# Diagonal matrices from GpSimd to VectorE, weight remainders to GpSimd, a third place for scores, contiguous q, k, v, and another order, in a fused attention and gated feed-forward kernel

## The chip, the core and the metric

The kernel runs on one core of a Trainium2 chip. A core has TensorE (PE: matmuls; PEld is its weight load), VectorE (DVE), ScalarE (ACT), GpSimd (POOL) and SyncE (SP, which here issues nearly all DMAs). The metric is the device time of one execution in microseconds. Three runs of the kernel before gave 413.46, 413.92 and 414.34 us.

## The reference

Three layers follow each other: windowed attention (4 batches, 8 heads, 576 positions, 64 wide; each query sees itself and the 63 keys before it), a token-shift feed-forward layer with a gate, and a convolution-gated layer.

```python
scores = scale * np.matmul(q, k.transpose(0, 1, 3, 2))
mask = (rel >= 0) & (rel < window)                 # window = 64
scores = np.where(mask, scores, -1000000000.0)
scores = scores - np.max(scores, axis=-1, keepdims=True)
attn = np.exp(scores)
attn = attn / (np.sum(attn, axis=-1, keepdims=True) + 1e-09)
x = np.matmul(attn, v)                             # then heads side by side: (4, 576, 512)

xk = mu_k * x + (1.0 - mu_k) * x_prev              # x_prev: x one position earlier
xr = mu_r * x + (1.0 - mu_r) * x_prev
k = np.maximum(xk @ w_k, 0.0)                      # 512 -> 1024
x = 1.0 / (1.0 + np.exp(-(xr @ w_r))) * (k * k @ w_v)

gate_pre += conv_w[k] * xp[:, k:k + S, :]          # 5 taps
x = (sigmoid(gate_pre) * (x @ w_val)) @ w_out
```

## The kernel before

The 2304 positions are cut into five blocks: block 0 of 256 and blocks 1 to 4 of 512. Attention runs in units: one block and one pair of heads, so four units a block, 0 to 3 for block 0, 4 to 7 for block 1, and so on. x lies with its features across partitions (tile xT).

A unit of block 0 takes these steps. The scores (qk, PE) come with the mask added by small matmuls of the tile low. DVE takes each row's maximum (top), ACT the exponentials and their sums (exp), POOL or DVE adds 1e-9 (eps), DVE takes the reciprocal (rec). A diagonal matrix of the reciprocals is made from the identity (diag, L446 to L455): as one DVE instruction over 4x128 columns (L453) or as four POOL instructions of 128x128 (L451). A matmul with it transposes and scales the weights (tp, L499), a copy brings them to SBUF (pt, L505, L506), a matmul with v gives the output (pv, L513), and a copy puts it into xT (x, L462, L463). Later units mask with DVE and a small memset on POOL (edge, L571), scale with norm (L442, L439) and transpose on DVE (tr).

The mixed inputs of block 0 are made by ACT (a) and DVE (xm, L643), for r and for k, in two groups of two head pairs. The products r, h (its relu squared) and v follow on PE: for block 0 in plain f32 from the weights' own words (L706), for blocks 1 to 4 as three products of halves: a weight is rounded (hi, L372, L373), and the remainder (lo, L375) is the difference of the weight and its rounded half. Weights come as 64-bit words in ten pieces (w_r two, w_k four, w_v four) that each need g (ACT, L351), t and s (DVE, L354, L356), hi and lo, all on 128x1024 elements. Block 0 needs a piece's s; blocks 1 to 4 need hi and lo. The last layer follows, by Strassen's scheme for three of four batches.

The table SLOT gives each operation its place in one order for the whole kernel, and a letter (v, a, p) the engine where there is a choice (v is DVE, a ACT, p POOL). Each engine's instructions, and SP's DMAs, stand in that order, so an engine that waits holds up all that it has later in the order. Plan.run goes through the order with a model of times, which decides one thing only: where it thinks that PE would idle before the first product it puts in filler matmuls (fill; the L1272 instructions).

In PSUM, the scores of units 0 to 4 take turns in two places (p0), and unit 5 has a third (s4). Products of later stages take over p0's banks at pg, when the exponentials of units 0 to 4 are done.

Of the kernel before, what the change touches and what calls it, by code (L numbers as in the profile page):

```python
# [20 lines left out]
P = 128  # L21
# [22 lines left out]
    'first': '0',  # L44
    'warm': '1',
    'cap': '3',
    'ident': '2',
    'band': '13',
    'low': '4',
    'table': '12',  # L50
    'ldmu': '7',
    'ldc': '92',
    'mu': '51',
    'omu': '52',
    'pg': '79',
    'wc0': '323 250 326',
    'wc': '327',
    'first_x': '6',
    'ldqk': '8 9 10 14 16 49 101 127 161 150 195 256 328 338 367 414 406 433 461 528',
    'ldv': '15 30 60 68 87 110 139 181 289 235 305 322 386 390 432 453 507 505 550 607',  # L60
    'qk': '18 21 22 36 45 69 103 148 187 241 257 337 350 373 389 431 452 508 520 540',
    'top': '19 23 29 53 62 77 140 178 262 267 283 347 366 404 422 443 460 524 541 554',
    'exp': '20 25 33 55 71 78 147 191 269 281 297 355 375 408 428 454 468 531 552 557',
    'eps': 'v24 p26 v41 p59 p88 p112 p175 p192 v270 v282 v311 p365 v380 v410 p439 v464 p488 p543 p558 p565',
    'rec': '27 35 50 64 91 138 176 198 271 285 312 368 381 411 447 466 516 544 568 583',
    'diag': 'v28 p40 p57 p67',
    'tp': '34 44 61 73',
    'pt': 'v37 a46 v66 v82',
    'pv': '38 48 70 83 128 166 200 223 294 313 356 378 412 436 481 499 535 563 573 614',
    'x': 'v47 a56 v81 a84 a136 a182 a216 a238 v298 a317 a357 v384 v415 v444 a486 a502 a536 a567 a578 a643',  # L70
    'norm': 'v95 v154 v179 v215 v272 v306 a340 a371 a382 a426 v448 v495 v517 v545 v569 v595',
    'tr': '96 158 184 219 273 308 348 372 399 427 449 496 533 551 572 604',
    'mask': '107 160 194 246 274 344 354 374 405 434 459 513 534 553',
    'edge': '126 171 218 264 280 345 360 376 413 437',
    'a': 'a65 a85 a89 a113 a225 a228 a244 a248 a333 v334 a392 v393 a465 v471 a521 v523 a605 a610 a686 v711',
    'xm': '75 98 108 114 236 237 277 251 349 346 403 395 478 476 547 538 622 663 690 738',
    'xlo': '76 100 137 120 240 243 321 255 364 391 441 397 512 518 587 577 677 708 724 783',
    'carry': '118 123 278 295 363 420 522 570',
    'r': '80 105 86 121 93 119 102 116 336 339 342 352 462 483 501 494 655 695 681 692 801 824 826 827',
    'sig': '115 124 129 135 341 358 370 388 477 487 515 519 676 696 697 698 816 825 837 838',  # L80
    'h': '149 153 146 159 143 151 145 152 169 177 174 189 185 196 183 197 290 287 268 279 296 307 314 302 '
        '416 435 407 421 450 467 463 479 599 594 600 611 618 613 667 653 749 748 778 766 780 784 804 818',
    'relu': 'a155 a163 a157 a162 a204 a205 a206 a210 a291 a292 a286 a293 v318 v320 a331 a332 a442 a451 a429 '
        'v430 a474 a485 v484 a497 a602 v603 v617 a624 a649 v657 a668 v669 a756 v758 a779 a791 a793 v796 '
        'a817 a821',
    'sbuf': '164 165 208 211',
    'slo': 'a202 a203 a209 a212 310 325 330 353 472 480 503 510 629 642 684 679 792 808 829 828',
    'v': '220 230 213 233 226 253 254 259 359 383 361 377 401 417 400 402 525 555 537 561 566 580 514 532 '
        '712 735 699 710 706 720 747 752 866 884 831 851 843 853 860 882',
    'x2': '263 247 258 260 387 379 425 409 559 571 588 564 742 723 733 763 892 888 887 889',  # L90
    'st': '276 284 369 303 418 398 445 473 575 584 630 582 769 743 772 774 950 959 1000 987',
    'xhi': 'a239 a242 v319 v252 v362 v385 v440 a396 a511 a500 a576 a546 a672 v700 a716 v757',
    'cut': '232 249 343 394 475 530',
    'shi': '300 315 324 335 456 457 491 498 621 625 660 670 762 795 797 822',
    'sq': 'a301 a316 v329 a351 v469 a470 a492 v506 v628 a627 a683 a678 a777 v805 a819 v823',
    'staging': '5',
    'w_r ld': '11 42',
    'w_r g': '32 58',
    'w_r t': '31 63',
    'w_r s': '39 72',  # L100
    'w_r hi': 'a43 v90',
    'w_r lo': '54 94',
    'w_k ld': '104 74 125 131',
# [12 lines left out]
    'turn': '836',
    'turn_s': '895',
    'turn_w': '865 845',
    'w_val ld': '542 562 597 647',
    'w_val room': '585 631 615 646',  # L120
    'w_val g': '586 633 619 654',
    'w_val t': '590 593 601 596 606 581 635 637 636 638 612 644 651 626 652 659 665 673 682 680',
    'w_val s': '592 634 620 661',
    'w_val hi': 'v608 a639 v662 a688',
    'w_val lo': '609 645 671 691',
    'w_val st': '616 632 648 658 666 675 717 705',
    'w_out ld': '640 694 740 746',
    'w_out room': '674 703 744 786',
    'w_out g': '687 704 745 787',
    'w_out t': '713 715 718 722 719 702 729 730 732 750 770 775 785 781 788 755 800 806 807 810',  # L130
    'w_out s': '714 721 771 798',
    'w_out hi': 'a726 v760 v789 a813',
    'w_out lo': '736 761 790 815',
    'w_out st': '759 751 767 773 809 802 814 835',
    'wv2': '867 839',
    'wo2': '902 880 881 848',
    'ldx': '841 904 926 1001',
    'gbuf': '871 922 1040 1034',
    'ldg': '873 949 1043',
    'xhi_': 'a846 v883 v855 a852 a879 a877 a910 a925 a909 a923 a948 a940 a972 a1056 a966 a982 a1002 a1009 a1075 '  # L140
        'a1106 a1077 a1090 v1124 v1105',
    'xlo_': '847 899 856 858 900 878 916 962 915 928 953 946 981 1061 991 983 1035 1021 1080 1118 1096 1102 '
        '1138 1110',
    'xsum': '842 849 859 876 906 911 924 934 958 964 994 1007 1070 1088 1103 1104',
    'val': '885 886 898 901 905 912 914 919 927 935 944 954 974 980 989 1066 999 1008 1028 1073 1044 1086 1098 '
        '1109 1114 1120 1135 1146',
    'valu': 'a891 a903 a907 a929 a945 a960 a996 a1016 a1031 a1100 a1112 a1127',
    'valc': '893 913 917 921 933 965 975 993 1068 1039 1082 1054 1108 1130 1140 1165',
    'gv': '894 920 918 932 973 978 986 1011 1069 1067 1089 1055 1164 1157 1142 1170',
    'ghi_': 'v896 a936 a930 a939 a943 a956 a967 a995 a1012 a1004 a992 a1006 a1022 a1025 a1093 a1062 a1101 v1113 '  # L150
        'a1116 v1144 a1132',
# [1179 lines left out]
```

## Time and profile before

| | |
|---|---|
| median of three runs | 413.92 us |
| the profiled execution: time, span | 413.41 us, 411.5 us |
| PE busy, share of the span | 402.6 us, 98% |
| DVE | 340.5 us, 83% |
| ACT | 261.5 us, 64% |
| POOL | 38.3 us, 9% |
| chain that ended last, by engine | PE 95%, POOL 3%, DVE 1% |
| moved by DMA | 78.37 MB |

The time of an execution is longer than its span, which runs from the first instruction on an engine to the last. A matmul's end is modelled, so that a busy PE is not a PE at its peak. Granted clock is the share of TensorE's full 2.4 GHz that the throttle allows. Idle time of an engine costs something only where another engine waits for it.

### The profile page before, as it was taken

Reading aid. Unit: us, or ns where it says so; the run is one execution under the profiler, and the core shown is the slowest. Engines: PE = TensorE matmul, PEld = TensorE weight load, DVE = VectorE, ACT = ScalarE, POOL = GpSimd, SP = SyncE. Lnnn points to the kernel's source line nnn. Section 1 sums busy time; section 2 is a strip of 40 time slices with the busy share of each in tenths; the row PEclk is TensorE's granted clock in tenths of the full one; section 3 lists DMA queues with packets and bytes.
Section 4 is the critical chain, followed back from the end, with each engine's and each line's share of the span. In section 5 each row is a group of like instructions: output and inputs, shape, how many; then the busy total and the mean of one; then the engine's idle time right before and its main releaser. Section 6 shows DMA issues by size and latency. Waiting matters only on the chain.

```text
span 411.5 us, 10921 instructions
## 1 busy us (share of the span) xinstructions
PE 402.6 (98%) x4587; PEld 342.1 (83%) x4587; DVE 340.5 (83%) x503; ACT 261.5 (64%) x607; POOL 38.3 (9%) x87
## 2 busy tenths in 40 slices
PE   8899999999999999999999999999999999999995
PEld 4678888887778778877888888888888999999995
DVE  4899999798548489789898899788885999999960
ACT  4889995778884767686556653156322476977531
POOL 3920101000100011000000000000000001123110
PEclk9999999999999999999999999999999999999999
DMA  7998911214323342262266428564999727869664
GB/s 284 411 414 339 328 46 57 78 44 145 107 74 129 98 125 77 78 223 92 80 242 263 149 89 291 208 235 156 405 395 382 261 86 245 228 142 198 137 149 128
DMA packets 24674, 78.37 MB, mean 190 GB/s; under 512 B 3376, under 2 KB 6704, under 8 KB 21808
## 3 DMA queue, kind: packets, MB, share of 16 engines
q1 hardware_dynamic: 22608, 72.64, 48.8%
q0 software_dynamic: 1872, 5.01, 7.3%
q8 instruction: 36, 0.59, 0.6%
q14 instruction: 14, 0.11, 0.1%
q10 hardware_dynamic: 144, 0.00, 0.0%
HBM read 51.80 MB, written 23.49 MB: 183 GB/s over the span
## 4 chain that ended last, share of the span: by engine, by line
PE 95%; POOL 3%; DVE 1%; ACT 0%; issue 0%; ACTq 0%; POOLq 0%
PE v L683 22%; PE h L683 21%; PE r L683 11%; PE sv L596 5%; PE h L706 4%; PE v L706 4%; PE sv L551 3%; PE val1m L961 3%; PE val3m L961 3%; PE out L1073 3%; PE out2m L961 3%; PE out1m L961 3%; PE val2m L961 3%; PE out0m L961 3%; PE val0m L961 3%; POOL rk L451 2%
## 5 line engine op out<-in xcount | busy, mean ns | idle before, releaser
L683 PE MATMUL h<-x,wk 128*128 128x512 f32 x384 | 90.5, 392 | 0.0
L683 PEld LDWEIGHTS h<-x,wk 128*128 128x128 f32 x384 | 71.6, 188 | 15.0
L683 PE MATMUL v<-sh,wv 128*128 128x512 f32 x256 | 82.4, 394 | 0.0
L683 PEld LDWEIGHTS v<-sh,wv 128*128 128x128 f32 x256 | 48.0, 188 | 10.8
L427 ACT ACTIVATE s<-s,m 128x96 f32<-128x96 f32 x120 | 43.0, 362 | 12.6 <-DVE m L416 11.5
L683 PE MATMUL v<-sl,wv 128*128 128x512 f32 x128 | 49.9, 390 | 0.0
L683 PE MATMUL r<-x,wr 128*128 128x512 f32 x192 | 45.8, 393 | 0.0
L683 PEld LDWEIGHTS r<-x,wr 128*128 128x128 f32 x192 | 35.7, 188 | 7.8
L892 DVE SCALAR_TENSOR_TENSOR early<-early,wc 128x576 f32<-128x576 f32 x48 | 38.5, 813 | 3.2 <-ACT early L890 2.7
L733 ACT ACTIVATE rk<-h 128x512 f32<-128x512 f32 (+1 forms) x30 | 15.4, 534 | 25.4 <-PE h L683 21.9
L683 PEld LDWEIGHTS v<-sl,wv 128*128 128x128 f32 x128 | 24.0, 188 | 4.7
L596 PEld LDWEIGHTS sv<-pt,vt 32*64 32x64 f32 x1536 | 18.9, 130 | 6.0 <-issue 3.9
L427 ACT ACTIVATION_READ_ACCUMULATOR s<-s,m 128x1 f32 x120 | 22.8, 190 | 0.0
L643 DVE SCALAR_TENSOR_TENSOR xm<-xT,omu,xm 128x512 f32<-128x512 f32 x32 | 22.3, 745 | 0.4 <-POOL xT L649 0.3
L666 DVE TENSOR_TENSOR x<-xm,x 128x1024 fp32r<-128x1024 f32 x16 | 19.5, 1219 | 3.6 <-ACT x L663 3.5
L785 DVE TENSOR_TENSOR sgs<-v,sgs 128x512 f32<-128x512 f32 (+1 forms) x20 | 12.5, 633 | 11.5 <-PE v L683 10.9
L763 DVE TENSOR_TENSOR sl<-rk,sh 128x1024 fp32r<-128x1024 f32 x16 | 19.5, 1221 | 2.4 <-ACT rk L761 2.2
L596 PE MATMUL sv<-pt,vt 32*64 32x32 f32 (+2 forms) x1536 | 20.8, 238 | 0.3 <-issue 0.3
L584 DVE STREAM_TRANSPOSE pt<-s 128x768 f32<-128x768 f32 x16 | 15.6, 973 | 5.1 <-ACT s L439 4.8
L757 ACT ACTIVATE sh<-rk 128x1024 fp32r<-128x1024 f32 x16 | 16.8, 1055 | 1.0 <-DVE rk L735 0.9
L896 ACT ACTIVATE early<-early 128x1152 f32<-128x1152 f32 x6 | 7.0, 1169 | 15.8 <-DVE early L892 15.8
L773 ACT ACTIVATE sgs<-r 128x512 f32<-128x512 f32 (+1 forms) x20 | 10.5, 552 | 8.2 <-PE r L683 8.1
(212 smaller groups left out, 828.0 us busy)
## 6 DMA issues: line engine op xcount, KB each, us to landing
qk<-qk SPq DMA_DIRECT2D x16, 544.0 KB, 5.1
vt<-vh SPq DMA_DIRECT2D x16, 384.0 KB, 3.9
xb<-x2d SPq DMA_DIRECT2D x4, 1152.0 KB, 6.7
out_t<-st SPq DMA_DIRECT2D x15, 288.0 KB, 2.9
w_out<-w SPq DMA_DIRECT2D x8, 512.0 KB, 3.4
w_val<-w SPq DMA_DIRECT2D x8, 448.0 KB, 3.1
wk<-w_val SPq DMA_DIRECT2D x2, 1792.0 KB, 8.8
early<-x2d SPq DMA_DIRECT2D x6, 576.0 KB, 4.4
```

The costliest lines, as they stand in the source:

```text
L427: ACT.activation(out=s, in_=scores()[:, 2 * c // n_s, c % (n_s // 2), :] if scores else s, func=AF.Exp, scale=D ** -0.5 if scores else 1.0 ...
L584: V.transpose(out=a["pt"][:, :m2 * KW], in_=a["s"].rearrange("p c j -> p (c j)"))
L596: PE.matmul(a["o"][heads[h], i, j0 * HW:j1 * HW], lhsT=a["v"][r, k, heads[h]], rhs=p, start=k == 0, stop=k == m + 1, skip_group_check=True)
L643: V.scalar_tensor_tensor(out=m, in0=xT[:, f, :n], scalar=omu[:, c:c + 1], in1=m, op0=ALU.mult, op1=ALU.add)
L666: lambda E: E.tensor_tensor(out=dst(1), in0=src(), in1=f32(dst(0)), op=ALU.subtract))
L683: PE.matmul(ps, lhsT=a, rhs=b[:, kt, :], start=(kt == 0 and i == 0), stop=(kt == nk - 1 and i == 2))
L706: PE.matmul(Ps[key][:, :n], lhsT=ws(kt), rhs=x()[:, kt, :], start=kt == 0, stop=kt == nk - 1)
L733: ACT.activation(out=o, in_=ps, func=AF.Relu)
L757: ACT.activation(out=Ss[t][0][:, f, :n], in_=rk(), func=AF.Square)
L763: lambda E: E.tensor_tensor(out=Ss[t][1][:, f, :n], in0=rk(), in1=f32(Ss[t][0][:, f, :n]), op=ALU.subtract))
L892: V.scalar_tensor_tensor(out=o, in0=x, scalar=c, in1=o, op0=ALU.mult, op1=ALU.add)
L961: PE.matmul(z[bank][:, j, :HS], lhsT=lhs, rhs=rhs, start=new and kt == 0 and e == 0, stop=kt == 1 and e == 2, skip_group_check=not new)
```

## The change

All four diagonals are made on DVE (the code offers ACT instead; the order takes DVE). lo may stand on POOL, and does for six of the ten pieces. The scores of the six early units go through three places in turn, p0, p0 and s4, by the unit's number; so unit 2 goes to s4, and unit 5 follows it there. pg then waits for the exponentials of units 0 and 3 alone, and the third and fourth r tile for those of 1 and 4. tp no longer waits for pv of the unit before; the copy pt does. Fillers write to the tp or pv places. The host lays out q with k, and v, so that what a unit loads is one contiguous stretch of memory; each DMA moves the same bytes to the same partitions. And nearly every place in SLOT is new. Of the table four entries are shown.

```diff
-    'ldqk': '8 9 10 14 16 49 101 127 161 150 195 256 328 338 367 414 406 433 461 528',
+    'ldqk': '9 11 12 15 16 64 82 102 146 170 252 260 306 362 353 374 382 440 477 509',
-    'diag': 'v28 p40 p57 p67',
+    'diag': 'v27 v42 v49 v62',
-    'w_r lo': '54 94',
+    'w_r lo': 'p69 p116',
-    'w_k lo': '180 144 227 229',
+    'w_k lo': 'v224 p203 p232 v226',
...
-    RAMP, STALL = 3500, 1300
+    STALLS = ((3500, 2000), (17500, 1100))
...
-        vg((key, "lo"), n, [(key, "hi")],
-           lambda E: E.tensor_tensor(out=dst[1], in0=s(), in1=f32(dst[0]), op=ALU.subtract))
+        rest = lambda E: E.tensor_tensor(out=dst[1], in0=s(), in1=f32(dst[0]), op=ALU.subtract)
+        plan.any((key, "lo"), [(key, "hi")], ("dve", v_ns(n), lambda: rest(V)), ("pool", 8000, lambda: rest(G)))
...
+    def unit_rows(a, o, hp, n):
+        return a[o + hp * P * n:][:P * n].rearrange("(p n) -> p n", p=P)
...
-            o = 2 * t0 + W * t
-            DMA.dma_start(out=both[:, :2 * n + W], in_=qkh[hp, :, o:o + 2 * n + W])
+            DMA.dma_start(out=both[:, :2 * n + W], in_=unit_rows(qkh, HP * P * (2 * t0 + W * t), hp, 2 * n + W))
...
+        def by_act():
+            d = diag()
+            for c in range(n_s):
+                ACT.activation(out=d[:, c], in_=ident, func=AF.Copy, scale=l(1)[:, c:c + 1])
         plan.any(("diag", u), [("rec", u), "ident", *free],
-                 ("pool", 1300, lambda: [G.tensor_scalar(out=o, in0=ident, scalar1=l(1)[:, c:c + 1], scalar2=None, op0=ALU.mult)
-                                         for o in [diag()] for c, o in enumerate([o[:, c] for c in range(n_s)])]),
+                 ("act", 290 * n_s, by_act),
...
+    def space(u):
+        return Q["s4"] if u % 3 == 2 else p0.tile([P, 2, TB], F32, tag="p0", name=f"qk{u}")
...
-            a["ps"] = p0.tile([P, 2, TB], F32, tag="p0", name=f"qk{u}")
+            a["ps"] = space(u)
...
-        op(("tp", u), "pe", 870, [("diag", u), *([("pv", u - 1)] if u else [])], tp, ring=("pa", ("pt", u)))
+        op(("tp", u), "pe", 870, [("diag", u)], tp, ring=("pa", ("pt", u)))
...
-        plan.any(("pt", u), [("tp", u)],
+        plan.any(("pt", u), [("tp", u), *([("pv", u - 1)] if u else [])],
...
-    op("pg", "none", 0, [("exp", u) for u in range(HP + 1)], products)
+    op("pg", "none", 0, [("exp", 0), ("exp", 3), After(("exp", 1)), After(("exp", 4))], products)
...
-        if "pg" in Q:
-            if "spare" not in Q:
-                Q["spare"] = Q["pg"].tile([P, TB], F32, tag="g", name="spare")
-            ps = Q["spare"]
-        elif "ps" not in A[HP + 1]:
-            ps = Q["s4"][:, 0]
-        elif len(held) < 2:
-            ps = Q["pv" if "tp" in held else "tp"]
-        else:
+        if "sv" in Q or len(held) > 1:
             return
+        ps = Q["pv" if "tp" in held else "tp"]
```

On POOL, from the masks of the start on, the order before is this (first_m and m4, m5 are the sums to which eps adds, rk the diagonals, s6 and s7 the scores whose mask is finished by memsets):

```order
L324 COPY band_96<-cap_95 32x96 x4
L432 TENSOR_SCALAR first_m_99<-first_m_99 128x4
L451 TENSOR_SCALAR rk_71<-ident_58,first_m_99 128x128 x8
L432 TENSOR_SCALAR first_m_99<-first_m_99 128x4
L451 TENSOR_SCALAR rk_71<-ident_58,first_m_99 128x128 x4
L432 TENSOR_SCALAR m4_364<-m4_364 128x8
L432 TENSOR_SCALAR m5_449<-m5_449 128x8
L571 MEMSET s6_549 32x2x64
L571 MEMSET s6_549 32x2x32
L571 MEMSET s7_711 32x2x64
L571 MEMSET s7_711 32x2x32
```

At the same place on POOL the new order has (wr1 and wk1 are the remainders of w_r and w_k; s8 is the next unit's mask):

```order
L442 TENSOR_SCALAR first_m_99<-first_m_99 128x4 x3
L331 COPY band_96<-cap_95 32x96 x4
L442 TENSOR_SCALAR m4_323<-m4_323 128x8
L381 TENSOR_TENSOR wr1_66<-words_119,wr0_65 128x4x256
L587 MEMSET s6_539 32x2x64
L587 MEMSET s6_539 32x2x32
L381 TENSOR_TENSOR wr1_66<-words_119,wr0_65 128x4x256
L587 MEMSET s7_667 32x2x64
L587 MEMSET s7_667 32x2x32
L381 TENSOR_TENSOR wk1_64<-words_119,wk0_63 128x4x256
L665 MEMSET xT_100 128x2
L587 MEMSET s8_832 32x2x64
```

The twelve diagonal instructions are gone from POOL, and remainders stand between the memsets of successive units.

On DVE, the last instructions ahead of the first mixing pair (the one that the first r product needs; rk is a diagonal, tp the transposed weights, words and x, s here the weight pieces, m the maxima of a later unit) are before:

```order
L375 TENSOR_TENSOR wr_66<-words,wr_65 128x4x256
L418 TENSOR_REDUCE m_364<-qk_285 128x8
L419 TENSOR_SCALAR m_364<-m_364 128x8
L354 TENSOR_SCALAR s_140<-s_140 128x1024
L435 RECIPROCAL first_m<-first_m 128x4
L506 COPY pt_359<-tp 128x512
L356 SCALAR_TENSOR_TENSOR words<-words,s_140 128x1024
L643 SCALAR_TENSOR_TENSOR x_139<-xT,omu,x_139 128x256 x2
```

The new order of DVE ends there with these:

```order
L466 TENSOR_TENSOR rk<-ident,first_m 128x512
L522 COPY pt_331<-tp 128x512
L361 TENSOR_SCALAR x_117<-x_117 128x1024
L445 RECIPROCAL first_m<-first_m 128x4
L363 SCALAR_TENSOR_TENSOR words<-words,x_117 128x1024
L478 COPY xT<-pv 128x256
L380 CAST wr_65<-words 128x4x256
L466 TENSOR_TENSOR rk<-ident,first_m 128x512
L428 TENSOR_REDUCE m_440<-s_143 128x8
L429 TENSOR_SCALAR m_440<-m_440 128x8
L659 SCALAR_TENSOR_TENSOR x_117<-xT,omu,x_117 128x256 x2
```

The diagonals (L466) are on DVE ahead of the pair, the remainder of the first w_r piece and the words of the second are no longer there, and the maxima of unit 5 (m_440) are.

On SP, which issues the loads, the first DMAs are before (x_139 and s_140 are the places of the two w_r pieces, early and qk units' q and k, sgs and rk their v):

```order
L400 DMA early<-qk 128x576 x3
L369 DMA x_139<-w_r 128x2048
L400 DMA early<-qk 128x576
L406 DMA sgs<-vh 128x512
L400 DMA qk_154<-qk 128x1088
L406 DMA sgs<-vh 128x512
L369 DMA s_140<-w_r 128x2048
```

And in the new order:

```order
L410 DMA early<-qk 128x576 x4
L410 DMA qk_173<-qk 128x1088
L415 DMA sgs<-vh 128x512
L376 DMA x_117<-w_r 128x2048
L415 DMA rk<-vh 128x512
L415 DMA sgs<-vh 128x512
L410 DMA qk_375<-qk 128x1088
L376 DMA s_118<-w_r 128x2048
```

The first w_r piece has moved behind the loads of units 3 and 4 and the first v.

## Rows read from the trace of the kernel before

**Rows 1.** Stages: PE, PEld, DVE, ACT, POOL busy us (x), PEclk, DMA, GB/s.
```profile
10.00:15.00 5.00, 4.24 (x105) 3.00 (x108) 4.82 (x11) 3.89 (x12) 4.39 (x5) 1.00 1.02 414
15.00:20.00 5.00, 4.35 (x149) 3.24 (x136) 3.58 (x6) 5.00 (x24) 4.54 (x7) 1.00 1.03 408
20.00:25.00 5.00, 4.57 (x49) 3.55 (x44) 4.82 (x10) 3.91 (x25) 2.23 (x4) 1.00 1.03 420
...
50.00:60.00 10.00, 10.00 (x227) 8.48 (x227) 9.84 (x11) 9.72 (x15) 0.12 (x2) 1.00 0.27 89
```

**Rows 2.** The chain that ended last, in order of time: start us, us, what.
```profile
10.61 2.67 POOL rk L451 x3
...
13.82 3.93 POOL rk L451 x4
...
18.41 3.63 POOL rk L451 x4
...
22.08 0.49 PE tp L499 x2
22.57 0.86 PE r L706 x4
23.43 0.62 PE pv L513 x16
...
26.84 0.93 PE sv L551 x56
...
42.01 0.30 issue
...
69.72 10.92 PE h L683 x48
```

**Rows 3.** Timeline of PE, first product: start, us, engine, line, op, tiles, count.
```profile
22.40 0.38 PE L706 MATMUL r<-x,words 128*128 128x256 f32 x1
```

**Rows 4.** Groups by line and form, POOL, 0 to 70 us: busy us, mean ns.
```profile
L451 POOL TENSOR_SCALAR rk<-ident,first_m 128x128 f32<-128x128 f32 x12 | 10.8, 911 | 1.4 <-DVE first_m L435 1.1 <-PE tp L499 0.4
...
L432 POOL TENSOR_SCALAR first_m<-first_m 128x4 f32<-128x4 f32 x2 | 0.4, 196 | 5.3 <-ACT xm L427 5.2
```

**Rows 5.** The same groups of DVE, 0 to 70 us.
```profile
L375 DVE TENSOR_TENSOR wk<-words,wk 128x1024 fp32r<-128x1024 f32 x4 | 4.8, 1211 | 0.0
...
L354 DVE TENSOR_SCALAR words<-words 128x1024 int32<-128x1024 int32 x4 | 2.7, 690 | 0.0
...
L356 DVE SCALAR_TENSOR_TENSOR words<-words,x 128x1024 int32<-128x1024 int32 x2 | 2.4, 1217 | 0.0
...
L506 DVE COPY pt<-tp 128x512 f32<-128x512 f32 x3 | 2.0, 682 | 0.2
...
L418 DVE TENSOR_REDUCE m<-qk 128x8 f32<-128x768 f32 x1 | 1.0, 959 | 0.5 <-PE qk L551 0.5
...
L453 DVE TENSOR_TENSOR rk<-ident,first_m 128x512 f32<-128x512 f32 x1 | 0.7, 691 | 0.0
```

**Rows 6.** Timeline of POOL, two of the twelve diagonal instructions.
```profile
12.67 0.60 POOL L451 TENSOR_SCALAR rk<-ident,first_m 128x128 f32<-128x128 f32 x1
...
18.98 1.64 POOL L451 TENSOR_SCALAR rk<-ident,first_m 128x128 f32<-128x128 f32 x1
```

**Rows 7.** Timeline of DVE, beside the second of those.
```profile
18.93 1.22 DVE L356 SCALAR_TENSOR_TENSOR words<-words,s 128x1024 int32<-128x1024 int32 x1
...
20.07 0.60 DVE L643 SCALAR_TENSOR_TENSOR x<-xT,omu,x 128x256 f32<-128x256 f32 x1
...
20.59 0.47 DVE L643 SCALAR_TENSOR_TENSOR x<-xT,omu,x 128x256 f32<-128x256 f32 x1
```

**Rows 8.** Timeline of DVE and PE: last w_v words, and their reader.
```profile
63.08 1.22 DVE L356 SCALAR_TENSOR_TENSOR rk<-rk,s 128x1024 int32<-128x1024 int32 x1
...
64.98 1.24 PE L706 MATMUL v<-s,rk 128*128 128x256 f32 x5
```

**Rows 9.** DMA issues: KB each, median us from issue (here at 2.11) to landing.
```profile
x<-w_r SPq DMA_DIRECT2D x1, 1024.0 KB, 7.6
```

More of the change, by code (lines that the diff above doesn't have):

```diff
@@ L218, in run @@
         for (key, _, deps, ring, tab, moves), w in self.ordered():
-            ready = [*deps]
+            ready = [d for d in deps if not isinstance(d, After)]
+            assert all(d.key in end for d in deps if isinstance(d, After))
             if ring and len(used[ring[0]]) >= self.rings[ring[0]]:
@@ L235, in run @@
                 new = max(link, end[key] + self.START) + moves
-                link = new + self.STALL * (link < self.RAMP <= new)
+                link = new + sum(n for at, n in self.STALLS if link < at <= new)
                 end[key] = link + self.LAND
@@ L404, in load_v @@
             a["v"] = home("vt", 2 * TB)[:, :nv * P].rearrange("p (c d) -> p c d", d=P)
-            c0 = t0 // P + 2 * t
-            DMA.dma_start(out=a["v"], in_=vh[:, hp, c0:c0 + nv, :])
+            DMA.dma_start(out=a["v"].rearrange("p c d -> p (c d)"),
+                          in_=unit_rows(vh, HP * P * P * (t and TA // W + (t0 - TA) // P + 2 * (t - 1)), hp, nv * P))
         op(("ldv", u), "dma", 420, back("pv"), load_v, moves=156.8 * nv)
@@ L487, in qk @@
                               rhs=a["k"][heads[h], c * W:c * W + P], start=False, stop=True, skip_group_check=True)
-        op(("qk", u), "pe", 728, [("ldqk", u), "low", "idle"], qk, ring=("p0", ("exp", u)))
+        op(("qk", u), "pe", 728, [("ldqk", u), "low", "idle"], qk, ring=("p0" if u % 3 < 2 else "s4", ("exp", u)))
         def s_of():
@@ L535, in qk @@
         def qk():
-            a["ps"] = Q["sv"] if not early_scores else Q["s4"] if u > HP else p0.tile([P, 2, TB], F32, tag="p0", name=f"qk{u}")
+            a["ps"] = Q["sv"] if not early_scores else space(u)
             if early_scores:
@@ L554, in unit @@
         if early_scores:
-            op(("qk", u), "pe", 1360, [("ldqk", u), "low", "idle"], qk, ring=("s4" if u > HP else "p0", ("exp", u)))
+            op(("qk", u), "pe", 1360, [("ldqk", u), "low", "idle"], qk, ring=("p0" if u % 3 < 2 else "s4", ("exp", u)))
         else:
@@ L767, in r_tile @@
         product(("r", t, m), wr, lambda: X[t]["r"],
-                lambda c: [("xlo", t, g, "r") for g in ((0, 1) if t else (c,))] + [(("w_r", m // 2), "lo" if t else "s")],
+                lambda c: [("xlo", t, g, "r") for g in ((0, 1) if t else (c,))] + [(("w_r", m // 2), "lo" if t else "s")]
+                + ([("exp", 1), ("exp", 4), *[After(("r", 0, i, 0)) for i in range(2)]] if t == 0 and m > 1 and c == 0 else []),
                 ("sig", t, m))
@@ L1299 @@
     kp[:, :, W:] = heads(k)
-    qk = np.concatenate([a for t0, n in BLOCKS for a in (qh[:, :, t0:t0 + n], kp[:, :, t0:t0 + n + W])], axis=2)
+    qk = np.concatenate([np.concatenate([qh[:, :, t0:t0 + n], kp[:, :, t0:t0 + n + W]], axis=2).reshape(-1) for t0, n in BLOCKS])
     vp = np.zeros((W + NT, DM), v.dtype)
     vp[W:] = v.transpose(0, 2, 1, 3).reshape(NT, DM)
-    vh = [np.stack([vp[g * W:g * W + P] for g in range(TA // W)]).reshape(-1, P, HP, P).transpose(1, 2, 0, 3)]
+    vh = [np.stack([vp[g * W:g * W + P] for g in range(TA // W)]).reshape(-1, P, HP, P).transpose(2, 1, 0, 3)]
     for t0, n in BLOCKS[1:]:
         g = np.stack([vp[t0 + i * (n // 4):][:n // 4 + W].reshape(-1, HW, HP, P) for i in range(4)])
-        vh.append(g.transpose(0, 2, 3, 1, 4).reshape(P, HP, -1, P))
-    vh = np.concatenate(vh, axis=2)
+        vh.append(g.transpose(3, 0, 2, 1, 4))
+    vh = np.concatenate([a.reshape(-1) for a in vh])
     cols = lambda a: np.asarray(a).reshape(-1, P).T
```

9 lines of the change are left out of this document (6 added, 3 removed), and 248 rows, old and new, of the table SLOT.

## The prediction

> **What bounds the kernel now.** I read the stages first [rows 1]. TensorE (PE) is busy 4.24 of 5 us between 10 and 15 us, part of that with filler matmuls, 4.57 between 20 and 25, and all of a later stage (50 to 60); the granted clock is 1.00, the 2.4 GHz level, in each. VectorE (DVE) is busy 3.58 of 5 us between 15 and 20, and nearly full from 20 us on (4.82 of 5, 9.84 of 10). Then the chain [rows 2]: from 10.61 to 22.04 us it goes through GpSimd (POOL), which writes the diagonal matrices of units 1 to 3 (2.67 + 3.93 + 3.63 us), and at 22.57 into the first product of x with w_r. From there PE alone stands in it, with one wait over 0.1 us (0.30, at 42.01), to its last product; an eviction and a store end the span at 411.5. So the time is three pieces: when the first product starts (22.40 us [rows 3]), PE's work behind it, which the change leaves as it is, and PE's waits in it. All working is against the profiled execution: 413.41 us, 1.91 more than its span. The median shown, 413.92, is 0.51 above it; I add that at the end.
>
> **Diagonals.** A diagonal is four 128x128 instructions on POOL, 911 ns each on average [rows 4], and one of 0.69 us on DVE [rows 5]. Three move to DVE, so POOL's 10.2 us leave the chain. Next late is DVE itself. Its order up to the first diagonal, done at 8.91, stays. Between it and the pair of mixing instructions that the first product waits for, the new order has 20 instructions: four maxima of 0.68 or 0.95, four scalings and three reciprocals and so on of 0.17, three diagonals of 0.69, two copies of tp of 0.68, the words of the first w_r piece (0.69, 1.22) and their rounding (0.68), a copy of 0.42: 10.9 us, the long ones by rows 5. Instructions that follow each other without a wait overlap by 0.08 (18.93 + 1.22 against 20.07 in rows 7): 20 x 0.08 back, so 9.3. With the pair (2 x 0.49) the end is 8.83 + 9.3 + 0.9 = 19.0 at the earliest. To that I add two waits. Instructions that read their predecessor's result lose the overlap, some ten times, 0.8 in all. And the maxima of unit 5 wait for PE: the second unit's tp copy ends on DVE at about 14.35; behind it PE has four fillers (some 0.25 each), pv (0.62), tp (four of 0.25), the scores of unit 5 (0.93, with some 0.2 of mask matmuls ahead), so they are there at 18.3, when DVE has been idle 0.55. That gives 20.4, and the first product at 20.5 instead of 22.40: 1.9 sooner. In the kernel before the same mixing pair was done at 21.06 [rows 7], and PE came to the product 1.3 later because tp of unit 3, ahead of it in PE's order, waited for POOL: the new order is no longer held there.
>
> **Remainders.** The order has six of them on POOL (two each of w_r, w_k, w_v), not four. DVE's 1.22 us each [rows 5] leave it, 7.3 us. They do not leave DVE shorter: it takes other work instead. From the first mixing pair to the words of the last w_v piece, DVE has 56 instructions before and 61 after; three remainders go (-3.6), and beside smaller things four scalings of 0.48 come (+1.9) and one words pair (+1.9): 0.9 to 1.3 us less in all. DVE starts the stretch 0.7 sooner, so it ends it 1.6 to 2.0 sooner, and PE comes 1.9 sooner. Before, those words ended at 64.30 and PE read them at 64.98 [rows 8]: slack 0.7, and about 0.6 of it stays. So DVE has nothing to give in that stretch: what POOL takes from it there, PE loses, beyond 0.6.
>
> What a remainder takes on POOL no row shows. A 128x128 instruction with one input takes 0.60 alone, a 128x4 one 0.20 [rows 4, 6], so 3.3 ns a column; 1024 columns are 3.6 us with one input, up to 7.2 with two. The readers are far: h of block 1 reads w_k's from 69.72 us [rows 2], r of block 1 w_r's later still, so even 7.2 each is hidden. Queued behind them on POOL are small memsets that finish the masks (the first two at about 27 and 35 us) and eps of later units; by the order the first follows a remainder that starts at 17.3, the second one that starts at 28.6: with 7.2 they are free at 24.5 and 35.8, so at worst the second costs 0.8 on a path with 1 us of slack. I cost that at nothing.
>
> The price that matters is DVE's. In rows 6 and 7 POOL's 128x128 instruction takes 1.64 instead of 0.60 when DVE's 1024-wide instruction, issued 0.05 sooner, runs: it ends 0.47 after it. DVE's next one, issued while POOL has its turn, takes 0.60 against 0.47 for its twin: DVE lost 0.12. So the loss per remainder is between nothing and 0.12 x 8 (columns) x 2 (inputs) = 1.9 us, if POOL's reading shuts DVE out for as long as it lasts. I take 0.12, the only hold that a row has, so 0.5 for the four remainders of that stretch, which the slack of 0.6 covers; 0.1 of it falls ahead of the first product and counts.
>
> The Trainium skill (SBUF — State Buffer, section Who interferes with whom) says that VectorE and GpSimd share a port pair as an exclusive lock: whoever is first has it for the whole instruction and the other fully blocks. The trace agrees for POOL (1.64 against 0.60), and for DVE only in part (0.12 of the 0.47 that POOL's instruction still ran). By that rule the sum is that of the first rival below. Its page GPSIMD Engine Reference (section Performance versus the Vector engine) gives 4497 ns for 2048 columns with two inputs, so an estimate of 2.2 us for 1024; by it the memsets are never late.
>
> **Scores, loads, the rest.** Unit 2's scores no longer wait for unit 0's exponentials: they start some 0.35 sooner, but DVE takes them only at 8.83, so 0. Contiguous q, k, v: the DMA engines are at 1.02 to 1.03 and 408 to 420 GB/s from 10 to 25 us [rows 1], with strided q, k, v and contiguous weights mixed, so nothing is left to win there; a loss has no mechanism in the rows. The queue's order moves, though: 1088 KB more stand ahead of w_r's first piece, at 414 GB/s 2.7 us, so it lands at 12.4 instead of 9.7 [rows 9]. DVE turns to it at 14.3; cover 1.9. Were it gone, each us late is a us late at the first product. Three more fillers run in idle time. Past 70 us PE has the same work and I leave 0.1 for a new small wait.
>
> **Sum.** 413.41 - 1.9 + 0.1 (port, ahead of the first product) + 0.1 (small waits) = 411.7 on the scale of the profiled execution, 412.2 on that of the median. By 0.2%, what can just be told from no change here, that is faster.
>
> **Rivals.**
> *The port is held through the whole read (slower).* Place: DVE between 17 and 62 us. For the four remainders there I look at what DVE has next in the order: maxima of PSUM data (it loses 0.3), mixing pair (1.9), maxima of SBUF data with one input and then words (1.0), scalings (1.9): 5.1, less 0.6 of slack, 4.5 on PE: 412.0 + 4.5 = 416.5. It decides from 0.6 us per remainder, where 4 x 0.6 less the slack has eaten the 1.9. For it: POOL was held for all of DVE's instruction, and some three quarters of DVE's time there is in instructions of such kinds (SBUF alone in and out). Against: one hold of 0.12 in the trace, and DVE instructions that start in the last 0.1 of a POOL one (18.93 in rows 6 and 7) take their usual 1.22. If POOL reads at 3.3 ns a column all the while, the holds are twice as long and the time is about 420.
> *Half of that (no change).* 0.5 to 0.8 per remainder, because POOL reads in the gaps: 413.1 to 414.7.
> *The start is not DVE's.* The loads come later than the byte count says, or PE's fillers, which now write into the tp buffer and so wait for its copy, push unit 5's scores back: the first product at 21.5 or later, 413.0 to 414.
>
> **How the numbers follow.** Forecast, gain of 0.9 to 3: 0.55. Its own range is 411.0 to 413.0; the low end is a first product at 19.2 (no waits of DVE), 413.92 - 3.0 = 410.9. No change, from the half hold or a late start that eats all: 0.13. Slower: 0.32, of it 0.22 for the held port at 414.8 to 417, 0.10 for worse. The range takes in the first rival's price and leaves out its tail: 410.9 to 417.0.
>
> **What would show it.** Right: the first r product at 20 to 21 us with DVE before it in the chain and no POOL; DVE's 1.22 us instructions beside a POOL remainder still 1.22; PE without a wait over 0.5 from there. The port rival: DVE's mixing, words and scaling instructions stretched by 1 to 2 us beside POOL's, PE waits on DVE between 35 and 66 us. Wrong altogether: PE waiting for a load ahead of 20 us, or for a memset on POOL between 35 and 50.

## The result, and the profile after

The changed kernel takes 418.63 us (median of 4 runs, 417.33 to 419.11), the kernel before in the same rounds 414.13; the ratio is 1.0102, with a 95% interval of 1.0072 to 1.0133. It is slower, by more than the range of the prediction (410.9 to 417.0) allowed. The first rival, the port that is held, named the mechanism, and priced it 2 us too low. The profiled execution took 419.11 us, with a span of 417.2 against 411.5.

The stages, in the columns of [rows 1]:

```profile
15.00:20.00 5.00, 4.62 (x125) 3.79 (x119) 4.59 (x7) 4.33 (x15) 3.01 (x2) 1.00 1.00 404
20.00:25.00 5.00, 4.67 (x48) 3.52 (x56) 4.89 (x9) 5.00 (x22) 0.00 (x0) 1.00 1.03 424
50.00:60.00 10.00, 6.71 (x122) 5.66 (x121) 10.00 (x12) 7.73 (x15) 5.98 (x4) 1.00 0.32 127
```

TensorE, full between 50 and 60 us before, is busy 6.71 of 10 now, with VectorE at 10.00 and GpSimd at 5.98. TensorE's timeline, those groups of matmuls that it came to late (in brackets how long it waited, and for what):

```profile
20.33 1.10 PE L722 MATMUL r<-x,words 128*128 128x256 f32 x4 [0.70 <-DVE x L659]
...
29.29 0.95 PE L612 MATMUL sv<-pt,vt 32*64 32x96 f32 x62 [1.00 <-issue]
...
37.11 1.28 PE L612 MATMUL sv<-pt,vt 32*64 32x32 f32 x96 [0.37 <-DVE s L578]
...
52.84 5.42 PE L722 MATMUL v<-s,early 128*128 128x256 f32 x24 [1.55 <-DVE early L363]
...
60.00 1.27 PE L612 MATMUL sv<-pt,vt 32*64 32x32 f32 x96 [1.74 <-issue]
...
73.18 3.01 PE L699 MATMUL h<-x,wk 128*128 128x512 f32 x12 [0.73 <-DVE sgs L802]
...
96.93 1.28 PE L612 MATMUL sv<-pt,vt 32*64 32x32 f32 x96 [0.61 <-DVE s L578]
```

The first r product starts at 20.33 us, where 20.5 was forecast and [rows 3] had 22.40; it waited for VectorE's mixing pair, and no GpSimd diagonal is in front of it. Behind it TensorE waits 7.3 us in ten places, where the kernel before had 0.36 in all. The wait at 60.00 is put down to nothing, but the transposed weights pt that these matmuls read leave VectorE at 59.89. Two of the ten are not VectorE's: the 1.00 at 29.29, in the midst of a group, and one of 0.14 at 92.34, for ScalarE.

The difference of the spans, 5.7 us, adds up: the start gives 2.07; the waits take 6.93; TensorE's busy time behind the first product grows by 1.85, most of it, by an estimate from the timeline, the ends of matmuls that nothing overlaps when a wait follows (a matmul takes 0.39 us and the next starts 0.23 after it, so 0.16 at each of ten waits); and the span ends 1.0 sooner behind the last matmul.

GpSimd's timeline, the six remainders:

```profile
17.40 2.37 POOL L381 TENSOR_TENSOR wr<-words,wr 128x1024 fp32r<-128x1024 f32 x1
...
27.85 2.53 POOL L381 TENSOR_TENSOR wr<-words,wr 128x1024 fp32r<-128x1024 f32 x1
...
40.74 2.36 POOL L381 TENSOR_TENSOR wk<-words,wk 128x1024 fp32r<-128x1024 f32 x1 [3.27 <-DVE wk L380]
...
52.21 5.58 POOL L381 TENSOR_TENSOR wk<-words,wk 128x1024 fp32r<-128x1024 f32 x1
...
68.90 2.39 POOL L381 TENSOR_TENSOR wv<-rk,wv 128x1024 fp32r<-128x1024 f32 x1
...
85.84 2.39 POOL L381 TENSOR_TENSOR wv<-early,wv 128x1024 fp32r<-128x1024 f32 x1 [2.33 <-issue]
```

And VectorE's, beside them:

```profile
17.64 0.96 DVE L428 TENSOR_REDUCE m<-s 128x8 f32<-128x768 f32 x1 [0.38 <-PE s L567]
18.63 1.16 DVE L429 TENSOR_SCALAR m<-m 128x8 f32<-128x8 f32 x1
...
28.07 2.34 DVE L442 TENSOR_SCALAR m<-m 128x8 f32<-128x8 f32 x1
...
41.37 2.27 DVE L361 TENSOR_SCALAR s<-s 128x1024 int32<-128x1024 int32 x1
...
54.35 1.21 DVE L363 SCALAR_TENSOR_TENSOR early<-early,x 128x1024 int32<-128x1024 int32 x1
55.49 3.52 DVE L659 SCALAR_TENSOR_TENSOR xm<-xT,omu,xm 128x512 f32<-128x512 f32 x2
...
68.34 3.50 DVE L659 SCALAR_TENSOR_TENSOR xm<-xT,omu,xm 128x512 f32<-128x512 f32 x2
...
85.85 3.20 DVE L452 TENSOR_TENSOR s<-s,m 128x768 f32<-128x768 f32 x1
```

A remainder takes GpSimd 2.4 us. In each, one VectorE instruction stands still: a scaling of 8 columns, 0.17 elsewhere, ends at 19.79, GpSimd's at 19.77; another of 0.15 takes 2.34 and ends at 30.41, GpSimd's at 30.38; the mixing pairs take 3.5 instead of 1.4. The six lose 1.0, 2.2, 1.6, 2.1, 2.1 and 2.2 us, 11.2 in all, for 7.3 (6 x 1.22) taken off VectorE. The maxima at 17.64 kept their time. At 52.21 it is the other way round: VectorE was running, instruction behind instruction, and GpSimd's remainder got its turn only at about 55.4 (5.58 us instead of 2.4).

### The profile page after: what moved, and what is told of

It is laid out like the page before. It is cut to its first block, busy times and chain, and to the rows that moved or that the text cites. A ratio compares the mean times of both kernels' runs of the same rounds, so it can differ in the third digit from the quotient of the medians.

```text
span 417.2 us, 10901 instructions
## 1 busy us (share of the span) xinstructions
PE 402.7 (97%) x4590; PEld 340.9 (82%) x4590; DVE 353.0 (85%) x515; ACT 250.2 (60%) x577; POOL 45.5 (11%) x82
## 4 chain that ended last, share of the span: by engine, by line
PE 73%; DVE 4%; DMA 2%; ACT 0%; issue 0%; ACTq 0%; DVEq 0%
PE v L699 21%; PE h L699 17%; PE r L699 11%; PE sv L612 3%; PE val1m L978 3%; PE val3m L978 3%; PE out L1090 3%; PE out1m L978 3%; PE val2m L978 3%; PE out2m L978 3%; PE out0m L978 2%; DMA xb<-x2d 2%; PE sv L567 2%; DVE s L452 1%; DVE rk L776 1%; DVE x L875 0%
## 5 line engine op out<-in xcount | busy, mean ns | idle before, releaser
L659 DVE SCALAR_TENSOR_TENSOR xm<-xT,omu,xm 128x512 f32<-128x512 f32 x32 | 26.5, 871 | 0.0
L578 DVE SCALAR_TENSOR_TENSOR s<-sv,band 128x768 f32<-128x768 f32 x14 | 13.3, 948 | 8.1 <-PE sv L567 7.3
```

Source lines behind the costliest of these rows:

```text
L578: V.scalar_tensor_tensor(out=a["s"], in0=ps, scalar=D ** -0.5, in1=band[:, None, :].to_broadcast([P, m2, KW]), op0=ALU.mult, op1=ALU.min)
L659: V.scalar_tensor_tensor(out=m, in0=xT[:, f, :n], scalar=omu[:, c:c + 1], in1=m, op0=ALU.mult, op1=ALU.add)
```

## The experiments

The theory, called port theory in the expectations (port stands for the way into SBUF, the on-chip memory, which the theory takes the two engines to share): what GpSimd reads for a remainder shuts VectorE out for that long, and VectorE, full from 17 to 62 us, passes it on to TensorE. The rival, called order theory: the new order itself makes TensorE wait. Ratios are to the kernel before, run in the same rounds.

**All remainders on VectorE.** Same order, same fillers.

```diff
-("pool", 8000, lambda: rest(G))
+("pool", 8000, lambda: rest(V))
```

> The changed kernel with its six POOL remainders issued on VectorE, at the same places of the order; nothing else differs. Port theory: beside each POOL remainder one VectorE instruction stood still until it ended, and lost 1.0 + 2.2 + 1.6 + 2.1 + 2.1 + 2.2 = 11.2 us in the six; on VectorE they cost 6 x 1.22 = 7.3. So VectorE gets 3.9 us back, TensorE's waits behind the first product fall from 7.3 to 3 to 5 us, and the time is 414.5 to 417. Order theory (the rest of the change, above all the new order, makes TensorE wait, whatever engine the remainders are on): VectorE now has 7.3 us more of its own work, 419 or more.

413.74 us, 1.0029 (1.0014 to 1.0043), a little below the range that the theory gave, and far from the rival's. TensorE's waits:

```profile
29.50 0.95 PE L612 MATMUL sv<-pt,vt 32*64 32x96 f32 x62 [0.99 <-issue]
...
53.43 3.72 PE L722 MATMUL v<-s,early 128*128 128x256 f32 x16 [0.33 <-DVE early L363]
...
65.57 1.99 PE L722 MATMUL v<-s,rk 128*128 128x256 f32 x8 [0.70 <-DVE rk L363]
...
92.95 1.28 PE L612 MATMUL sv<-pt,vt 32*64 32x32 f32 x96 [0.64 <-DVE s L578]
```

They fall from 7.3 to 3.1 us. Moving the six to GpSimd, the one thing that differs, costs 1.0102 against 1.0029, 3.0 us. Without it the change is still not faster than the kernel before, so the rest of the change has a part too: 3.1 us of waits, against 0.36, outweigh a first product at 20.55 us, 1.85 sooner.

**GpSimd writes but doesn't read.**

```diff
-("pool", 8000, lambda: rest(G))
+("pool", 8000, lambda: G.memset(f32(dst[1]), 0.0))
```

> The changed kernel in which POOL's six remainders are memsets of the same 128x1024 elements: the subtraction is left out, so POOL reads nothing there. Port theory in the form that POOL's reading holds VectorE: no VectorE instruction is stretched, TensorE's waits fall from 7.3 to 1.5 at most, 412 to 413.5 (what the prediction gave with almost no hold). If a write of POOL holds VectorE as well: stretched by as long as the memset takes, 414 to 418. Order theory: 418 to 419.

409.98 us, 0.9936 (0.9913 to 0.9960), below every range given, and 0.5 us of waits in all; the first product at 20.01. GpSimd, then VectorE:

```profile
27.39 0.96 POOL L382 MEMSET wr<- 128x1024 f32 x1
...
48.15 0.96 POOL L382 MEMSET wk<- 128x1024 f32 x1
```

```profile
27.63 0.75 DVE L442 TENSOR_SCALAR m<-m 128x8 f32<-128x8 f32 x1
...
47.44 1.23 DVE L363 SCALAR_TENSOR_TENSOR early<-early,words 128x1024 int32<-128x1024 int32 x1
48.57 1.09 DVE L361 TENSOR_SCALAR x<-x 128x1024 int32<-128x1024 int32 x1
```

Not quite as either theory had it: a write alone does hold VectorE's quick kind (0.75 for 0.15 to 0.17, 1.09 for 0.69), but not the instruction with two inputs (1.23 as ever). The loss is 1.0 us. This run shows also what the rest of the change is worth once the six remainders cost next to nothing: 2.6 us. The same order with them on VectorE was at 1.0029, so 7.3 us of VectorE's work are 3.8 us of TensorE's time.

**GpSimd reads one input.**

```diff
-("pool", 8000, lambda: rest(G))
+("pool", 8000, lambda: G.tensor_copy(dst[1], s()))
```

> The changed kernel in which each POOL remainder is a copy of its first input, 128x1024 (the second input and the subtraction are left out). If one read of POOL holds VectorE like two do, VectorE instructions beside it are stretched until its end (by the copy's own time, 1 to 2.4 us), the scalar ones and the mixing ones with two inputs alike, and TensorE waits 2 to 6 us: 413 to 418. If only two inputs hold it: only the 0.69 us kind is stretched, as beside the memsets, by up to a microsecond, 410 to 413.

412.2 us in a single run, the kernel before at 413.7. Two of GpSimd's copies, the first of which found the ports free, and VectorE's words beside the two:

```profile
36.18 1.04 POOL L382 CAST wk<-words 128x1024 fp32r<-128x1024 f32 x1 [0.86 <-DVE words L363]
...
49.73 3.13 POOL L382 CAST wk<-words 128x1024 fp32r<-128x1024 f32 x1
```

```profile
36.30 2.00 DVE L363 SCALAR_TENSOR_TENSOR words<-words,x 128x1024 int32<-128x1024 int32 x1
...
51.88 2.06 DVE L363 SCALAR_TENSOR_TENSOR early<-early,x 128x1024 int32<-128x1024 int32 x1
```

One input holds two-input instructions too, for 0.78 to 0.86 us: 3.3 us in all over four of the six. So one read holds as two do, for less than half as long; the time, of one run, lies in the range given for the other case. TensorE's first r product in this run, where nothing held VectorE ahead of it:

```profile
19.62 1.03 PE L722 MATMUL r<-x,words 128*128 128x256 f32 x4
```

**The remainders in eighths.**

```diff
-("pool", 8000, lambda: rest(G))
+("pool", 8000, lambda: [G.tensor_tensor(out=dst[1][c], in0=s()[c], in1=f32(dst[0][c]), op=ALU.subtract)
+    for k in range(nk) for m in range(0, nm, P) for c in [(slice(None), k, slice(m, m + P))]])
```

> The changed kernel with each POOL remainder cut into eight instructions of 128x128; the same elements in all. Port theory: the hold lasts one instruction, so VectorE gets in between the pieces: its loss is no more than 0.3 us at a time, but can come up to eight times per remainder; I expect half of the 11.2 us and 416 to 417. If VectorE loses the same in all, 418 to 419.5. Order theory: no change, 418.6.

413.58 us, 1.0020 (1.0000 to 1.0039): faster than expected. VectorE loses 5.7 us, 0.2 to 0.3 at a time, half as foreseen, and GpSimd gets through more slowly, 4.6 to 9.8 us a remainder:

```profile
28.37 6.14 POOL L382 TENSOR_TENSOR wr<-words,wr 128x128 fp32r<-128x128 f32 x8
```

```profile
30.20 1.16 DVE L659 SCALAR_TENSOR_TENSOR x<-xT,omu,x 128x256 f32<-128x256 f32 x2
31.28 0.95 DVE L361 TENSOR_SCALAR x<-x 128x1024 int32<-128x1024 int32 x1
```

So the hold is that of one instruction, and ends with it. That takes back as much as keeping the remainders on VectorE.

**Four remainders on GpSimd in the kernel before.**

```diff
+        POOL_LO = {("w_k", 1), ("w_k", 2), ("w_v", 2), ("w_v", 3)}
...
-           lambda E: E.tensor_tensor(out=dst[1], in0=s(), in1=f32(dst[0]), op=ALU.subtract))
+           lambda E: (G if key in POOL_LO else E).tensor_tensor(out=dst[1], in0=s(), in1=f32(dst[0]), op=ALU.subtract))
```

> The kernel before with four of its remainders on POOL (the second and third of w_k, the third and fourth of w_v), at their places in the order; nothing else of the change. Port theory: each takes 1.22 us from VectorE and gives back a hold of up to 2.3, so two cost VectorE up to 2.2 ahead of the end of block 0, where it has 0.6 to spare: 414 to 416. Order theory: VectorE is freed of 4.9 us and nothing else changes, 413 to 414.

416.24 us, 1.0078 (1.0051 to 1.0106): the hold is there in the old order too, but what TensorE waits for is something else. VectorE beside the first of the four (at 33.47 for 2.37 us), TensorE, and the stages with the granted clock:

```profile
33.51 2.89 DVE L373 CAST wk<-words 128x1024 fp32r<-128x1024 f32 x1
```

```profile
36.18 0.41 PE L551 MATMUL sv<-qk 64*32 64x96 f32 x17 [0.48 <-issue]
...
41.03 1.23 PE L596 MATMUL sv<-pt,vt 32*64 32x32 f32 x91
44.05 0.31 PE L596 MATMUL sv<-pt,vt 32*64 32x32 f32 x5 [1.78 <-issue]
44.28 3.33 PE L706 MATMUL h<-x,words 128*128 128x256 f32 x8
```

```profile
42.00:46.00 4.00, 2.22 (x35) 1.80 (x24) 3.90 (x6) 2.22 (x4) 0.00 (x0) 0.85 0.82 262
46.00:50.00 4.00, 4.00 (x15) 3.29 (x15) 2.85 (x4) 4.00 (x20) 0.20 (x1) 0.73 0.97 368
```

VectorE lost 2.2, 1.2, 2.1 and 1.6 us at the four, but neither of TensorE's two waits behind the first product is for it. The 0.48 comes behind 47 of 64 matmuls of a group; the run with the diagonals alone, below, waits 1.00 in that group with no remainder on GpSimd. The 1.78 comes behind 91 of 96 matmuls, where the kernel before waited its 0.30 [rows 2]. The clock falls to 0.85 and 0.73 behind it: eight products take 3.33 us, 0.42 each, against 0.23 for the 24 at 52.84 in the changed kernel. So this run shows the hold, and not that it costs TensorE anything there.

**Diagonals back to GpSimd**, in the new order, with the remainders on VectorE.

```diff
-                 ("dve", v_ns(n_s * P), lambda: V.tensor_tensor(
+                 ("dve", v_ns(n_s * P), lambda: [G.tensor_scalar(out=o, in0=ident, scalar1=l(1)[:, c:c + 1], scalar2=None, op0=ALU.mult)
+                     for o in [diag()] for c, o in enumerate([o[:, c] for c in range(n_s)])] if u else V.tensor_tensor(
```

> The kernel with the remainders on VectorE (413.74 us, first r product at 20.55 us) in which the diagonals of units 1 to 3 go back to GpSimd, four 128x128 instructions each, at their places in the new order. Theory of the prediction (the start was GpSimd's diagonals): each takes 2.4 to 3.9 us instead of 0.69 in the chain that leads to the first product, which comes at 22 to 23 us; VectorE has 2.1 us less to do behind it, so of the 1.5 to 2.5 us some comes back: 414.5 to 416. Rival (the start was gained by the new order and the third place for scores): first product at 21 at the latest, 413 to 414.

417.92 us, 1.0108 (1.0084 to 1.0131): 3.3 us slower than with the diagonals on VectorE, more than expected. GpSimd's three diagonals, VectorE's mixing pair, and the first product:

```profile
11.49 2.35 POOL L466 TENSOR_SCALAR rk<-ident,first_m 128x128 f32<-128x128 f32 x4
...
14.21 3.88 POOL L466 TENSOR_SCALAR rk<-ident,first_m 128x128 f32<-128x128 f32 x4
18.05 2.50 POOL L331 COPY band<-cap 32x96 f32<-32x96 f32 x4
20.64 2.94 POOL L466 TENSOR_SCALAR rk<-ident,first_m 128x128 f32<-128x128 f32 x4
```

```profile
21.52 0.98 DVE L659 SCALAR_TENSOR_TENSOR x<-xT,omu,x 128x256 f32<-128x256 f32 x2
```

```profile
23.96 1.03 PE L722 MATMUL r<-x,words 128*128 128x256 f32 x4
```

It starts at 23.96 instead of 20.55. Not all of that is the diagonals': the new order has four copies for the masks ahead of the third one, 2.50 us on GpSimd, and VectorE's pair was done at 22.50. Without the copies an estimate from these rows is 22.6, within the theory's range and clear of the rival's. VectorE's freed 2.1 us brought nothing back.

**The diagonals alone**, in the kernel before.

```diff
-    'diag': 'v28 p40 p57 p67',
+    'diag': 'v28 v40 v57 v67',
```

> The kernel before with its three GpSimd diagonals on VectorE, at their places in the old order; nothing else of the change. Theory (the diagonals were the chain at the start, but VectorE takes their place): first product at 21.0 to 21.8 us instead of 22.4, VectorE has 2.1 us more to do behind it, of which 0.6 is slack: 412.5 to 414.5 against 413 to 414, no change. Rival (the diagonals alone are the gain): 1 to 2 us faster.

414.99 us, 1.0018 (0.9997 to 1.0039), no change, as expected, if 0.5 above the range. But the first product came at 22.30, not at 21.0 to 21.8. VectorE's mixing pair was done at 20.75; ahead of the product stood four fillers, which the planner put there since the diagonals' times had changed, and which in the old code write to a place that scores still hold:

```profile
21.45 1.02 PE L1272 MATMUL spare<-sgs 128*128 128x512 bf16 x4 [0.55 <-ACT s L427]
22.30 1.03 PE L706 MATMUL r<-x,words 128*128 128x256 f32 x4
```

What the diagonals alone would give without these fillers stays open; the gain of 2.07 needed more of the change than them.

**The old layout of q, k, v**, with the remainders on VectorE (the host's arrays and the two DMAs as in the kernel before).

> The kernel with the remainders on VectorE, with q, k, v laid out in memory as in the kernel before (strided rows). Theory of the prediction: the loads' rate between 10 and 25 us is that of the engines either way, so no change, 413.2 to 414.3. Rival: the strided loads land later by 0.5 us or more ahead of 20 us, and the first product with them, 414.3 or more.

414.48 us, 1.0021 (1.0005 to 1.0038) beside 1.0029 with the new layout; first product at 20.58 and 20.55. The median is just above the range, as the kernel before was slower too in these rounds (413.70 for 412.78). The layout does nothing that can be told.

**Three tries to mend the rest**, all from the kernel with the remainders on VectorE. The first changes VectorE's order:

```diff
-    'w_k lo': 'v224 p203 p232 v226',  'w_v s': '200 208 211 243',  'w_v lo': 'v347 v270 p294 p264',
+    'w_k lo': 'v224 p212 p232 v226',  'w_v s': '200 208 211 230',  'w_v lo': 'v347 v270 p346 p264',
```

> The kernel with the remainders on VectorE, with three of VectorE's places in the order changed: the remainder of the second w_k piece goes behind the words of the third w_v piece, the words of the fourth w_v piece come ahead of the remainder of the third w_k piece, and the remainder of the third w_v piece goes later by some ten instructions. TensorE waited 0.33, 0.70 and 0.64 us for what stood behind those three remainders. Theory (VectorE's order sets those waits): they go, 1.7 us less, 411.5 to 412.6, no slower than the kernel before. Rival (what is pushed back, the mixed inputs of block 1, is as late): 413 to 414.

416.56 us, 1.0078 (1.0054 to 1.0101), worse than either expectation. The three waits went, and others came, 3.1 us of them, among these:

```profile
57.12 1.27 PE L612 MATMUL sv<-pt,vt 32*64 32x32 f32 x96 [0.72 <-ACT wk L379]
...
80.66 3.04 PE L699 MATMUL h<-x,wk 128*128 128x512 f32 x12 [1.26 <-DVE sgs L802]
```

What this order brought forward on a full VectorE it made late elsewhere. The second takes work off VectorE; the third has a153 and a171 besides:

```diff
-    'w_k hi': 'a221 v153 v195 a222',
+    'w_k hi': 'a221 v153 a195 a222',
...
-    a108 v171 v196 a239      (in 'a')
+    a108 v171 a196 a239
...
-    a275 v303 v317 a318      (in 'relu')
+    a275 a303 a317 a318
```

> The kernel with the remainders on VectorE, with four pieces of VectorE's work moved to ScalarE at their places in the order: the rounding of the third w_k piece, one pair of scaled inputs (a), and two relus of block 1; 2.8 us in all. Theory (VectorE is the bound between 17 and 95 us, and ScalarE has idle time there): TensorE's waits of 0.33, 0.70 and 0.64 us go or shrink, 411.5 to 413, by 0.2 to 0.5% less than that kernel's 413.74. Rival (ScalarE is as late, since it is the other half of the same chains): 413.5 to 415.

> As the last, and two more pieces on ScalarE, earlier: the rounding of the second w_k piece and another pair of scaled inputs, 1.5 us, between 36 and 43 us, where ScalarE has exponentials to do. Theory: VectorE gains 1.5 us, but ScalarE was busy 8 to 9 of 10 us there, so little more than the last: 411.5 to 413. Rival: exponentials come late by 1 to 2 us, and TensorE with them: 414 to 415.5.

The second: 413.84 us, 1.0010 (0.9994 to 1.0026), 2.8 us of waits, the rival's side. The third: 418.16 us, 1.0112 (1.0084 to 1.0141), worse than either expectation; ScalarE is late with a relu, TensorE waits 2.21 us for it, and its clock falls:

```profile
48.74 1.13 PE L722 MATMUL h<-x,words 128*128 128x256 f32 x4 [2.21 <-ACT rk L749]
```

```profile
50.00:54.00 4.00, 3.96 (x11) 3.27 (x12) 2.89 (x4) 3.97 (x8) 0.01 (x1) 0.59 0.52 200
```

The last joins the second with eighths on GpSimd for w_r and w_v, and w_k's remainders on VectorE:

> Two parts together: the remainders of w_r and w_v that were on GpSimd stay there in eighths, those of w_k go to VectorE, and the four pieces of the earlier run (one rounding, one pair a, two relus) are on ScalarE. By the stretches seen with eighths, the four remainders cost VectorE 0.5, 1.1, 0.5 and 0.9 us instead of 1.22 each, so it has 1.9 us less to do than with all on VectorE. Theory (VectorE's sum sets TensorE's waits): they fall from 2.85 us to 1.5 to 2, 412 to 413, faster than the kernel before by 0.1 to 0.4%. Rival (the eighths stretch to 5 to 6 us on GpSimd and the memsets that finish the masks wait for them; or the load of instructions in the second group of sv matmuls stays as it is): no faster than the kernel before, 413.5 to 414.5.

414.04 us, 1.0015 (1.0000 to 1.0031), the rival's side. Its waits are 2.4 us, of them 0.77 in the group of sv matmuls at 28.5. No version that keeps the whole computation came out faster than the kernel before.

## Why the prediction was wrong, step by step

- **The start** was right in its mechanism: VectorE's mixing pair came last, and no GpSimd diagonal was in front. With the diagonals on GpSimd the first product is at 23.96, some 1.4 of it for the copies in between, so the gain needs them; in the old order, with fillers in the way, they gave 0.1. That the number came so close, 20.33 us for 20.5, is luck: the first remainder held VectorE for 1.0 ahead of the pair, where 0.1 was put, and VectorE's own chain was put too long by some 0.5 to 0.9. Where nothing held it the first product came at 19.62 (the copies) and 20.01 (the memsets).
- **The readers of the remainders, the memsets, the loads, the layout** were right: no wait stands on GpSimd or on a load ahead of 20 us, and the layout changes nothing. A remainder takes 2.4 us, below the bounds of 3.6 to 7.2: the 3.3 ns a column came from small instructions, most of whose time does not grow with the columns. The estimate from the Trainium skill (GPSIMD Engine Reference, section Performance versus the Vector engine), 2.2 us, was nearer. But for the hold, the sum was near: the memsets' 0.9936 comes to 411.3 us on the median of 413.92, where 412.2 was forecast.
- **The failed step is the price of a remainder to VectorE**: "I take 0.12, the only hold that a row has, so 0.5 for the four remainders of that stretch". It measured 1.0, 2.2, 1.6 and 2.1, so 6.9, and 11.2 with the two behind. The row was read rightly and carried over wrongly: 0.12 was the hold by 128 columns and one input, and I let it stand for 1024 columns and two. The working had the scaled number, 0.12 x 8 x 2 = 1.9, but as the far end of a range. One input of 1024 columns holds 0.8, two hold 2.1 to 2.2, eighths with two inputs 0.2 to 0.3 each: the hold goes by what GpSimd reads.
- **The argument against the rival failed too.** That instructions of 1.22 kept their time beside GpSimd's last 0.1 us says who came first, not that nobody waits; at 52.21 us VectorE, ahead, made GpSimd wait, and in the other five cases GpSimd was ahead of the instruction that it held. The Trainium skill (SBUF — State Buffer, section Who interferes with whom) has it that the first holds the shared ports for its whole instruction, that instructions with two inputs contend with GpSimd's reads alone, the fast one-input modes with its writes too, and reductions with neither. The runs agree with each: 2.11 lost by the mixing pair beside reads, 1.23 unchanged beside a memset, 0.69 turned into 1.09 beside it, and 0.96 for the maxima at 17.64. Only the whole instruction is too much for a small one: of the 0.47 that GpSimd's still ran, VectorE lost 0.12 [rows 6, 7]. It was the rule to go by.
- **The slack of 0.6** was read at one place, 64.98 us; TensorE waited for VectorE sooner, at 37.11 and 52.84. And the first rival's 416.5 was too low. It gave the four remainders 5.1 where VectorE lost 6.9 (0.3 for the first, which cost 1.0, since a scaling of 0.17 stood behind the maxima). It had nothing for the two behind, where VectorE lost 4.3 more: TensorE's waits from 70 to 100 us are 1.8, and 0.8 with the remainders on VectorE. And each wait costs TensorE 0.16 more than it lasts, by the estimate above.
- **Left out**: a wait of 1.0 in the second group of sv matmuls, and an end of the span 1.0 sooner. They cancel.

## What to carry to other kernels

Before work goes from VectorE to GpSimd, look at what VectorE does next at that place: if that reads SBUF with two inputs, or is a quick one-input instruction, the price is what is left of GpSimd's reading time, here 1.0 to 2.2 us for 1.22 saved. By these runs it pays only where VectorE is idle, or has a reduction or an instruction that reads PSUM. A price seen on a small instruction is scaled by columns and inputs before it is used. With VectorE full, orders that mended one wait made another, and moving 2.8 us of its work to ScalarE brought nothing that can be told; the only version clearly faster than the kernel before left the work out (the memsets).

## What the runs showed of the hardware

- Beside a GpSimd instruction that reads 1024 columns twice, VectorE instructions with two SBUF inputs or of the quick kind wait until its end (losses of 1.0 to 2.2 us); beside one that reads once, 0.8 to 0.9; beside one that only writes, up to 0.6 and the quick kind alone. A reduction beside two reads kept its 0.96 (at 17.64), and in the run in eighths a copy from PSUM its 0.41 (at 20.96). It works in both directions (5.58 us for 2.4 on GpSimd).
- TensorE can stop in the midst of a group of small matmuls with nothing in the profile to wait for, and it does so at the same places of its stream. Counted in weight loads of the trace, 486 stand ahead of the stop of 0.8 to 1.1 us in the changed kernel and seven of its versions. In the two versions of the kernel before, 615 stand ahead of those of 0.48 and 1.00; in it and them, 744 or 743 ahead of those of 0.30, 1.78 and 1.01. So the places lie 129 loads apart, which with as many matmuls is 258 instructions, whatever matmul stands there. In each case a load of queue q8 (kind instruction, 16 KB) had ended 1.2 to 1.6 us before TensorE went on; in the three versions that pass the first place without a stop (memsets, eighths, diagonals on GpSimd) it had ended 2.1 to 2.8 us before. That speaks for TensorE waiting for its instructions there. No run was made to test it, and why the load came sooner in some kernels stays open.
- After waits of 1.78 and 2.21 us the granted clock stood at 0.73 and 0.59 in a stretch of 4 us, between its levels of 1.2 and 2.4 GHz; in the profile of the changed kernel, with waits of 1.55 and 1.74, it stayed at 1.00.
